# Casting values in the load and packing keys-times-values in 64x64 quadrants: one change to a fused linear-attention and highway kernel

## The chip, the cores and the metric

The kernel runs on one NeuronCore of a Trainium2 chip. Five engines work beside each other and meet at semaphores: PE (TensorE, the matrix array, with its weight loads as PEld), DVE (VectorE), ACT (ScalarE), POOL (GpSimd) and SP (SyncE, which here only issues transfers). The metric is the device time in microseconds (us) of one execution. The kernel before takes 144.22 us, the median of three runs (143.59 to 144.29). The profile comes from one more execution.

## The reference, cut to what matters

```python
# q, k, v: (8 batches, 8 heads, 576 positions, 64), float32
q_s = exp(q - max over the last axis);  q_s /= sum over the last axis
k_s = exp(k - max over positions);      k_s /= sum over positions
kv  = einsum('bhsd,bhse->bhde', k_s, v)          # one 64x64 matrix for each head
x   = einsum('bhsd,bhde->bhse', q_s, kv)         # laid out as 4608 tokens x 512
H   = max(x @ w_h, 0);  T = 1 / (1 + exp(-(x @ w_t + b_t)))
out = T * H + (1 - T) * x                        # 4608 x 512, float32
```

The maxima cancel in the quotients, so the kernel takes plain exponentials and divides by sums that come out of the matrix products through a column of ones.

## The kernel before, in words

All work is written as short steps, and one long string, `ORDER`, gives the order in which they are issued. `v_2_0_4` is a step `v` for batch 2, starting at head pair 0, four pairs. A suffix chooses the engine (`:A` ACT, `:D` DVE, `:P` POOL; `th_9_0:S` writes in place). There is no scheduler behind it: an engine does its steps in the order of the string, and a step that waits holds up all that follows on that engine. The queue in which SP issues transfers goes in the same order.

For each of the eight batches:

- `k`, `v`, `q` load float32 values through SP (lines 168 and 174), into three buffers for each kind. Keys and values have 64 positions of one head on 64 partitions and 9 further positions (`NJ`) along the row, so two heads fill 128 partitions.
- `ek` (line 222, ACT) takes the exponential of the keys into fp16. `vc` (line 227, on ACT, DVE or POOL) copies the values to fp16 into `v16`, where each position has 64 values and, behind them, a one.
- `kv` (line 243, PE) makes keys times values: 144 products with 64 rows, 32 columns of weights and 65 moving columns. Even and odd key channels are separate products, so that each half lands on the 32 partitions that belong to its head. The result `kvps` is in the PSUM tile pool `ps_x`, which has one buffer; the products `xu` use the same buffer.
- `kr` and `kn` (lines 250 and 253, DVE) take the reciprocal of the sums and write the normalised matrix as fp16 into `kvb`.
- `eq` (line 260, ACT) takes the exponential of the queries, `tr` (line 278, DVE) transposes it in 32x32 blocks, `xu` (lines 291 and 301, PE) multiplies by `kvb` for a group of tokens, and `rs` and `x` (lines 313 and 319, DVE) divide by the sums and write the tokens as fp16.

For each of 36 tiles of 128 tokens: `xt` turns the tile on PE (line 326), `xe` copies it out (line 332, ACT or DVE), `bw` puts the bias into a PSUM bank (line 339 by ACT, line 341 by PE), `mt` and `mh` are four products each of 128x128 weights by 512 columns (lines 346 and 352), `th` is the tanh (lines 359 and 362, ACT), `dd`, `uu` and `oo` are the elementwise end (lines 366, 377 and 380, 392, on DVE or POOL), `gg` (line 371, POOL) prepares `uu` on POOL, and `st` and `st1` store (lines 401 and 413).

`fill` (line 155) issues products on an empty tile at the start, so that PE is busy while data is on its way. `setuppool` builds two identity matrices on POOL.

Of the kernel before, what the change touches and what calls it, by code (L numbers as in the profile page):

```python
# [16 lines left out]
b_32 b_0 setupdve fill_10 bsplit v_0_3_1 bp fill_10 v_0_0_1 v_0_2_1 vc_0_0_1:A bc vc_0_3_1:D k_0_2_2 ek_0_2_2 k_0_0_2  # L17
v_0_1_1 q_0_0_8 ek_0_0_2 vc_0_2_1:D bw_1_0 vc_0_1_1:D kv_0 w_t_0 wtc_0:P q_0_8_10 w_h_0 w_t_2 kr_0 eq_0_0_8 tr_0_0_8
w_h_2 kn_0 fill_4 xu_0 rs_0 x_0 setuppool bw_0_0 fill_4 xt_0 whd_1:D eq_0_8_10 whd_0:P tr_0_8_8 xe_0:A xt_1 wtc_2:P
k_1_0_2 xe_1:D whc_0:A xu_1 whd_2:D whd_3:P whc_2:A mt_1_0 th_1_0 mt_0_0 rs_1 x_1 xt_2 ek_1_0_2 v_1_2_2 xe_2:D  # L20
vc_1_2_2:P mh_0 dd_0 mh_2 th_0_0 gg_0_0:P mh_1 bw_2_0 dd_2 bw_3_0:A gg_1_0:P dd_1 v_1_0_2 k_1_2_2 ek_1_2_2 q_1_0_8
eq_1_0_8 xt_3 xe_3:D mt_2_0 vc_1_0_2:D uu_0_0:P mh_3 q_1_8_10 dd_3 oo_0_0:D mt_3_0 tr_1_0_8 uu_1_0:P oo_1_0:P th_2_0
k_2_0_4 gg_2_0:P kv_1 kr_1 kn_1 eq_1_8_10 tr_1_8_8 v_2_0_4 bw_4_0 th_3_0 uu_2_0:P bw_5_0:A xu_2 rs_2 x_2 xt_4 xu_3
ek_2_0_4 tr_0_16_2 oo_2_0:P gg_3_0:P xe_4:D uu_3_0:P rs_3 tr_1_16_2 x_3 xt_5 mt_4_0 xe_5:A mh_5 q_2_0_18 v_3_0_4
k_3_0_4 th_4_0 vc_2_2_2:D vc_2_0_2:A q_3_0_18 xt_6 oo_3_0:P xu_4 rs_4 gg_4_0:P x_4 q_4_0_18 xe_6:A mt_5_0 mh_4 th_5_0
dd_5 dd_4 xt_8 xe_8:D eq_2_0_8 tr_2_0_8 kv_2 kr_2 kn_2 bw_8_0:A gg_5_0:P mt_8_0 eq_2_8_10 tr_2_8_8 mh_6 bw_6_0:A xt_7
th_8_0 xe_7:D bw_7_0:A xu_5 mt_6_0 rs_5 uu_5_0:P dd_6 x_5 vc_3_0_2:A th_6_0:S v_4_0_4 mt_7_0 uu_6_0:D k_4_0_4 mh_7
dd_7 uu_4_0:P xu_6 rs_6 xt_10 xe_10:D th_7_0 oo_5_0:P ek_3_0_4 mh_8 mh_10 x_6 oo_4_0:P dd_8 xt_9 xe_9:D bw_10_0:A
mt_10_0 vc_3_2_2:P kv_3 dd_10 v_5_0_4 eq_3_0_8 tr_3_0_8 kr_3 oo_6_0:P gg_7_0:P uu_7_0:P eq_3_8_10 tr_3_16_2 bw_11_0:A
kn_3 oo_7_0:P xt_11 xe_11:A tr_2_16_2 mh_9 gg_8_0:P uu_8_0:P th_10_0 gg_10_0:P tr_3_8_8 xu_7 bw_9_0:A oo_8_0:P  # L30
eq_4_8_10 vc_4_2_2:P mt_11_0 th_11_0 mt_9_0 th_9_0:S q_5_0_18 uu_10_0:P bw_12_0:A k_5_0_4 rs_7 vc_4_0_2:P dd_9 x_7
eq_4_0_8 xt_12 xe_12:D mh_11 uu_9_0:D oo_9_0:P xu_8 rs_8 gg_11_0:P oo_10_0:P xt_13 xe_13:D dd_11 uu_11_0:P st_0
mt_12_0 xt_14 th_12_0 x_8 mh_12 gg_12_0:P bw_13_0:A mh_13 ek_4_0_4 xu_9 oo_11_0:P mt_13_0 th_13_0:S xe_14:D dd_12 rs_9
xt_15 x_9 q_6_0_18 bw_14_0 xe_15:A dd_13 kv_4 uu_12_0:P oo_12_0:P tr_4_0_8 k_6_0_4 kr_4 vc_5_0_2:A xt_16 xe_16:A
mt_14_0 uu_13_0:D mh_15 kn_4 xu_10 bw_16_0:A th_14_0 gg_14_0:P st_1 tr_4_8_8 dd_15 xt_17 mh_14 rs_10 xe_17:D eq_5_8_10
mt_16_0 vc_5_2_2:P v_6_0_4 bw_15_0:A mt_15_0 x_10 xt_18 dd_14 eq_5_0_8 tr_5_0_8 xu_11 th_16_0 bw_17_0 th_15_0:S
# [5 lines left out]
rs_14 mh_20 tr_6_8_8 th_22_0 oo_16_0:P bw_24_0:A xt_25 st1_17_0 oo_19_0:P gg_22_0:P x_14 gg_20_0:P dd_20 bw_21_0:A
uu_18_0:P st_6 vc_6_0_2:A mt_24_0 th_24_0 xe_25:D tr_6_0_8 mt_21_0 th_21_0:S kv_6 kr_6 uu_21_0:D kn_6 mh_22 dd_22
mh_25 dd_25 xu_15 ek_7_0_4 uu_20_0:P rs_15 x_15 bw_23_0:A mt_23_0 oo_18_0:P eq_7_0_8 tr_7_0_8 uu_22_0:P xt_26 mh_24
bw_25_0:A mt_25_0 st_8 dd_24 th_23_0 xu_16 gg_23_0:P rs_16 xe_26:A xt_28 xe_28:D bw_26_0:A mt_26_0 gg_24_0:P
vc_7_2_2:A oo_21_0:P vc_7_0_2:A x_16 oo_20_0:P st_7 th_25_0:S th_26_0 uu_25_0:D mh_23 gg_26_0:P xt_27 xe_27:A
eq_7_8_10 st_11 kv_7 oo_22_0:D kr_7 kn_7 uu_24_0:P mh_28 dd_23 dd_28 xt_29 mh_26 dd_26 xu_17 rs_17 xe_29:A xt_30
bw_29_0:A mt_29_0 x_17 bw_28_0:A oo_25_0:P mt_28_0 xe_30:A th_29_0 uu_23_0:P oo_24_0:P mh_27 oo_23_0:P st_10 tr_7_8_8
bw_27_0:A uu_26_0:P th_28_0:S uu_28_0:D xt_31 xe_31:A tr_7_16_2 dd_27 mt_27_0 bw_31_0:A th_27_0:S xt_32 xu_18
tr_6_16_2 rs_18 xe_32:A uu_27_0:D gg_29_0:P mt_31_0 x_18 oo_26_0:P th_31_0 mh_29 dd_29 mh_30 bw_30_0:A mt_30_0  # L50
oo_28_0:D bw_32_0:A st_13 oo_27_0:P st_12 uu_29_0:P gg_31_0:P dd_30 th_30_0:S xu_19 rs_19 oo_29_0:P uu_30_0:D
# [8 lines left out]
def kernel(  # L60
# [10 lines left out]
    nc = tc.nc  # L71
# [14 lines left out]
    ldv = pool("ldv", 3)  # L86
# [75 lines left out]
    def load_kv(which):  # L162
        src, p = (k, ldk) if which == "k" else (v, ldv)

        def step(e, b, c, n):
            t = landing(which, b, p).rearrange("p (c f) -> p c f", c=4)
            rows = src[b].rearrange("(c hh) (p j) d -> (hh p) c (j d)", hh=2, p=NP)
            nc.sync.dma_start(t[:, c:c + n], rows[:, c:c + n])  # L168
        return step
# [49 lines left out]
    def ek(e, b, c, n):  # L219
        t = once(f"ek{b}", lambda: ekp.tile([P, NJ, 4, D], FP16, tag="ek", name=f"ek_{b}"))  # L220
        src = T[f"k32{b}"].rearrange("p (c j d) -> p c j d", c=4, j=NJ)
        nc.scalar.activation(t[:, :, c:c + n].rearrange("p j c d -> p c j d"), src[:, c:c + n], AF.Exp)  # L222

    def vc(e, b, c, n):
        copy = dict(A=nc.scalar.copy, D=nc.vector.tensor_copy, P=nc.gpsimd.tensor_copy)[e or "P"]
        src = T[f"v32{b}"].rearrange("p (c j d) -> p c j d", c=4, j=NJ)
        copy(v16[b % NV][:, c:c + n, :, 0:D], src[:, c:c + n])  # L227

    def kv_of(b):
        return T[f"kvps{b}"][:, 0:2, 0:130].rearrange("p m (c e) -> p m c e", c=2)  # L230

    def kv(e, b):


        ps = T[f"kvps{b}"] = ps_x.tile([P, 4, DM], FP32, tag="xu", name=f"kv_{b}")
        for turn in range(2):
            for c in range(2):
                for j in range(NJ):
                    for g in range(4):
                        h = 4 * c + g  # L240
                        hh, i, m = h % 2, h // 2, (turn + h) % 2
                        rows, cols = slice(64 * hh, 64 * hh + 64), slice(32 * g, 32 * g + 32)
                        nc.tensor.matmul(  # L243
                            ps[cols, m, 65 * c:65 * c + 65], T[f"ek{b}"][rows, j, i, m:D:2],
                            v16[b % NV][rows, i, j, 0:65], start=(j == 0), stop=(j == NJ - 1),
                            skip_group_check=True, tile_position=(64 * hh, 32 * g))
# [208 lines left out]
```

## Time and profile before

| | value |
|---|---|
| median of three runs | 144.22 us |
| the profiled execution's own time | 142.23 us |
| its span, first to last instruction | 140.5 us |
| busy: PE, DVE, ACT, POOL | 112.2, 98.2, 90.9, 85.9 us |
| mean granted PE clock | 0.907 |
| read from HBM, written | 30.41 MB, 9.44 MB |
| keys times values (line 243), 1152 products | 12.5 us |
| casts of the values (line 227): ACT, POOL, DVE | 7.5, 5.7, 5.8 us |

The profile page cuts the span into 40 slices of 3.5 us. A digit of an engine's row is its busy share in tenths, PEclk is the clock that the throttle granted to TensorE, and DMA is the busy share of the 16 transfer engines. The chain of work is followed back from the last instruction, at each step to what released it; a piece of it called issue is time in which the engine waited for nothing that the profile names. In the groups of instructions, the last column is the idle time of the engine just before them and what ended it.

### The profile page before, as it was taken

To read this page: it belongs to the slowest core of one execution; us is meant where nothing else is said; L and a number is where in the kernel's file an instruction comes from. 1 tells how busy PE (TensorE), PEld (TensorE's weight loads), DVE (VectorE), ACT (ScalarE), POOL (GpSimd) and SP (SyncE) were. 2 spreads that over 40 slices of the span, in tenths; PEclk is the share of its full clock that TensorE was granted. 3 is DMA by queue.
4 is the path that set the end of the run, shared out by engine and by line. 5 is a ranking of instruction groups with operands and counts; after the bars stand their busy time and mean duration, and the time that the engine had idled before them with its cause. 6 is when DMAs were issued, how large, how long until landed. Compare 5 with 4: busy or idle time off the path is not lost.

```text
span 140.5 us, 5171 instructions
## 1 busy us (share of the span) xinstructions
PE 112.2 (80%) x2267; PEld 58.9 (42%) x2267; DVE 98.2 (70%) x176; ACT 90.9 (65%) x121; POOL 85.9 (61%) x93
## 2 busy tenths in 40 slices
PE   6947879936997599189923999399999999999930
PEld 2315245524364255035522456145565464544510
DVE  3703786977477597557923498287999999998890
ACT  3345376776577595916931689349999978866710
POOL 0001546999139469494980437903998879989930
PEclk9997899996599999959995599869999999999996
DMA  4999999999999999999999999100291052724362
GB/s 138 261 398 407 401 392 387 394 395 398 392 396 410 394 387 392 403 402 405 396 401 399 404 396 355 40 0 0 82 398 53 5 201 103 296 84 167 132 269 106
DMA packets 14890, 40.17 MB, mean 286 GB/s; under 512 B 914, under 2 KB 1170, under 8 KB 14868
## 3 DMA queue, kind: packets, MB, share of 16 engines
q1 hardware_dynamic: 14576, 39.59, 73.9%
q8 instruction: 17, 0.28, 0.8%
q10 hardware_dynamic: 292, 0.27, 0.6%
q14 instruction: 5, 0.04, 0.1%
HBM read 30.41 MB, written 9.44 MB: 284 GB/s over the span
## 4 chain that ended last, share of the span: by engine, by line
PE 63%; DVE 13%; issue 10%; DMA 6%; ACT 3%; SPq 2%; DVEq 0%
PE tps L346 22%; PE gps L352 21%; PE turned L326 7%; PE kv L243 7%; DMA v<-in_v_dram 6%; PE xu L291 4%; DVE d L366 3%; DVE et L278 3%; DVE x L319 2%; ACT qe L260 2%; DVE o L392 2%; SPq L168 2%; DVE v L227 1%; PE turned L155 1%; DVE xT L332 1%
## 5 line engine op out<-in xcount | busy, mean ns | idle before, releaser
L392 POOL TENSOR_TENSOR o<-u,x 128x512 f32<-128x512 f16 (+1 forms) x30 | 35.6, 1195 | 7.4 <-DVE u L377 6.8
L346 PE MATMUL tps<-w16t,xT 128*128 128x512 f16 (+1 forms) x148 | 39.7, 403 | 0.2 <-DVE xT L332 0.2
L352 PE MATMUL gps<-w16h,xT 128*128 128x512 f16 x144 | 38.5, 400 | 0.0
L380 POOL TENSOR_TENSOR u<-g,d 128x512 f16<-128x512 f16 x23 | 27.7, 1212 | 4.7 <-DVE d L366 4.2
L366 DVE SCALAR_TENSOR_TENSOR d<-x,gps 128x512 f16<-128x512 f16 x36 | 24.3, 679 | 4.8 <-PE gps L352 4.7
L371 POOL TENSOR_SCALAR g<-th 128x512 f16<-128x512 f16 x23 | 14.1, 618 | 20.3 <-ACT th L362 20.3
L260 ACT ACTIVATE qe<-q 128x1024 f16<-128x1024 f32 (+1 forms) x16 | 18.6, 1164 | 6.3 <-DVE kvb L253 1.9
L319 DVE TENSOR_TENSOR x<-xu,rs 128x1024 f16<-128x1024 f32 (+1 forms) x20 | 22.2, 1112 | 0.3
L278 DVE STREAM_TRANSPOSE et<-qe 128x512 f32<-128x512 f32 (+1 forms) x24 | 20.0, 835 | 2.9 <-ACT qe L260 2.9
L243 PE MATMUL kv<-v,ek 64*32 64x65 f16 x1152 | 12.5, 197 | 10.3 <-issue 7.3
L346 PEld LDWEIGHTS <-xT 128*128 128x128 f16 x148 | 14.0, 104 | 15.0 <-issue 3.7
L352 PEld LDWEIGHTS <-xT 128*128 128x128 f16 x144 | 13.8, 102 | 14.7 <-issue 2.8
L222 ACT ACTIVATE ek<-k 128x2304 f16<-128x2304 f32 (+1 forms) x10 | 17.4, 1736 | 3.5 <-DMA k<-in_k_dram 3.5
L339 ACT COPY tps<-ball 128x512 f32<-128x512 f32 x29 | 16.8, 592 | 3.3 <-DVE d L366 3.1
L362 ACT ACTIVATE th<-tps 128x512 f16<-128x512 f32 x23 | 13.6, 596 | 8.1 <-PE tps L346 8.0
L332 ACT COPY xT<-turned 128x512 f16<-128x512 f16 x18 | 10.6, 586 | 12.8 <-PE turned L326 12.8
L326 PE MATMUL turned<-idh,x 128*128 128x128 f16 x144 | 15.0, 231 | 4.0 <-DVE x L319 3.3
L243 PEld LDWEIGHTS <-ek 64*32 64x32 f16 x1152 | 11.0, 94 | 13.1 <-issue 8.2
L326 PEld LDWEIGHTS <-x 128*128 128x128 f16 x144 | 10.6, 102 | 11.1 <-DVE x L319 4.1
L291 PE MATMUL xu<-kvb,et 32*128 32x65 f16 x512 | 7.8, 197 | 6.9 <-issue 5.1
L359 ACT ACTIVATE tps<-tps 128x512 f32<-128x512 f32 (+1 forms) x14 | 7.7, 550 | 5.8 <-PE tps L346 5.5
L291 PEld LDWEIGHTS <-et 32*128 32x128 f16 x512 | 5.5, 97 | 13.6 <-issue 7.3
(42 smaller groups left out, 82.3 us busy)
## 6 DMA issues: line engine op xcount, KB each, us to landing
out_dram<-o SPq DMA_DIRECT2D x16, 512.0 KB, 5.6
k<-in_k_dram SPq DMA_DIRECT2D x6, 1152.0 KB, 14.5
v<-in_v_dram SPq DMA_DIRECT2D x6, 1152.0 KB, 16.1
q<-in_q_dram SPq DMA_DIRECT2D x6, 1152.0 KB, 15.3
k<-in_k_dram SPq DMA_DIRECT2D x4, 576.0 KB, 9.1
q<-in_q_dram SPq DMA_DIRECT2D x2, 640.0 KB, 12.1
v<-in_v_dram SPq DMA_DIRECT2D x4, 288.0 KB, 4.1
v<-in_v_dram SPq DMA_DIRECT2D x2, 576.0 KB, 11.5
```

What stands on the lines that cost most here:

```text
L222: nc.scalar.activation(t[:, :, c:c + n].rearrange("p j c d -> p c j d"), src[:, c:c + n], AF.Exp)
L243: nc.tensor.matmul(ps[cols, m, 65 * c:65 * c + 65], T[f"ek{b}"][rows, j, i, m:D:2], v16[b % NV][rows, i, j, 0:65], start=(j == 0), stop=(j ...
L260: nc.scalar.activation(t[:, :, j * D:(j + n) * D], src[:, :, j * D:(j + n) * D], AF.Exp)
L278: nc.vector.transpose(dst, src)
L291: nc.tensor.matmul(t[:, g, col:col + 65], turned_q(bs[0], c, m, 256 * J + P * a, P)(rows), kvb[bs[0] % NKV][rows, m, c, 0:65], start=(m == ...
L319: nc.vector.tensor_mul(dst[:, :, 0:n], sums(u)[:, :, :, 0:64], T[f"rs{u}"][:, :, 0:n].unsqueeze(3).to_broadcast([P, 4, n, D]))
L326: nc.tensor.matmul(t[:, n], x_of(i)[:, n0 + n % 2:n0 + 2 * P:2], idh, is_transpose=True, start=True, stop=True, skip_group_check=True)
L346: nc.tensor.matmul(T[f"tps{i}_{h}"][:, cs], T[f"xT{i}"][:, n], w16["t"][:, n, cs], start=False, stop=(n == 3), skip_group_check=True)
L352: nc.tensor.matmul(t, T[f"xT{i}"][:, n], w16["h"][:, n], start=(n == 0), stop=(n == 3), skip_group_check=True)
L366: nc.vector.scalar_tensor_tensor(t, x_of(i), -0.5, T[f"gps{i}"], op0=ALU.mult, op1=ALU.max)
L380: nc.gpsimd.tensor_mul(t[:, cs], T[f"g{i}_{h}"][:, cs], T[f"d{i}"][:, cs])
L392: eng.tensor_add(t[:, cs], T[f"u{i}_{h}"][:, cs], x_of(i)[:, cs])
```

## The change

Values are no longer loaded as float32 by SP and cast by a compute engine. POOL issues their loads itself, and the transfer writes fp16 straight into `v16`, of which there are now three. A row of `v16` holds the values of all positions, and at its end one block of 64 ones.

`kv` takes whole 64x64 quadrants: 72 products for a batch, each with 64 columns of weights and 128 moving columns, the 64 values of a position and the block of ones. To that end `ek` writes each position's even channels first and its odd ones behind them. Half of each result now lies on the neighbouring 32 partitions. After `kn`, the new step `kp` moves those halves by two products with a permutation matrix `swap` into a further bank of the same PSUM buffer, `kc` (ACT, once DVE) copies them to `kvm`, and `xu` takes each half from `kvb` or `kvm`. `perm` builds `swap` on POOL, ahead of the first load of values.

The order of all steps is new, loads and stores included. On PE the program shrinks from 4536 to 3418 instructions. Nine loads of values stand in POOL's order among its compute steps. Of the other choices of engine, `xe` has three more on ACT, `bw` two more on ACT in place of PE, `oo` one more on DVE in place of POOL, and a weight cast moves from POOL to ACT.

```diff
-b_32 b_0 setupdve fill_10 bsplit v_0_3_1 bp fill_10 v_0_0_1 v_0_2_1 vc_0_0_1:A bc vc_0_3_1:D k_0_2_2 ek_0_2_2 k_0_0_2
...
+q_0_8_10 b_0 b_32 eq_0_8_10 setupdve fill_10 bsplit setuppool perm k_0_0_2 k_0_2_2 ek_0_2_2 bp fill_12 bc bw_3_0
+v_0_2_2 tr_0_8_8 v_0_0_2 q_0_0_8 ek_0_0_2 kv_0 kr_0 kn_0 bw_2_0:A w_h_0 w_t_2 wtc_2:P eq_0_0_8 tr_0_0_8 fill_4 kp_0
+kc_0:A xu_1 rs_1 whd_0:D x_1 fill_5 xt_2 w_t_0 wtc_0:A xu_0 w_h_2 k_1_0_2 xe_2:D rs_0 k_1_2_2 xt_3 x_0 mt_2_0 whd_2:D
...
-    ldv = pool("ldv", 3)
-    NKV, NV = 3, 2
+    NKV, NV = 3, 3
-    v16 = [consts.tile([P, 4, NJ, 66], FP16, name=f"v16_{i}") for i in range(NV)]
+    kvm = [consts.tile([P, 2, 66], FP16, name=f"kvm{i}") for i in range(NKV)]
+    swap = consts.tile([P, 2, P], FP16, name="swap")
+    v16 = [consts.tile([P, 4 * NJ * D + D], FP16, name=f"v16_{i}") for i in range(NV)]
...
+    def perm(e):
+        nc.gpsimd.memset(swap, 0.0)
+        for to in range(4):
+            r, w = 32 * (to ^ 1), to % 2
+            nc.gpsimd.tensor_copy(swap[r:r + 32, w, 32 * to:32 * to + 32], idh[r:r + 32, r:r + 32])
...
-            nc.vector.memset(t[:, :, :, 64:66], 1.0)
+            nc.vector.memset(t[:, 4 * NJ * D:], 1.0)
...
+    def load_v(e, b, c, n):
+        w = NJ * D
+        t = v16[b % NV][:, c * w:(c + n) * w].rearrange("p (c f) -> p c f", c=n)
+        nc.gpsimd.dma_start(t, rows_of(v, b)[:, c:c + n])
...
     def ek(e, b, c, n):
-        t = once(f"ek{b}", lambda: ekp.tile([P, NJ, 4, D], FP16, tag="ek", name=f"ek_{b}"))
-        src = T[f"k32{b}"].rearrange("p (c j d) -> p c j d", c=4, j=NJ)
-        nc.scalar.activation(t[:, :, c:c + n].rearrange("p j c d -> p c j d"), src[:, c:c + n], AF.Exp)
-
-    def vc(e, b, c, n):
-        copy = dict(A=nc.scalar.copy, D=nc.vector.tensor_copy, P=nc.gpsimd.tensor_copy)[e or "P"]
-        src = T[f"v32{b}"].rearrange("p (c j d) -> p c j d", c=4, j=NJ)
-        copy(v16[b % NV][:, c:c + n, :, 0:D], src[:, c:c + n])
+        t = once(f"ek{b}", lambda: ekp.tile([P, 4 * NJ, D], FP16, tag="ek", name=f"ek_{b}"))
+        src = T[f"k32{b}"].rearrange("p (s r m) -> p s r m", s=4 * NJ, m=2)
+        dst = t.rearrange("p s (m r) -> p s r m", m=2)
+        at = slice(NJ * c, NJ * (c + n))
+        nc.scalar.activation(dst[:, at], src[:, at], AF.Exp)
...
-        for turn in range(2):
-            for c in range(2):
-                for j in range(NJ):
-                    for g in range(4):
-                        h = 4 * c + g
-                        hh, i, m = h % 2, h // 2, (turn + h) % 2
-                        rows, cols = slice(64 * hh, 64 * hh + 64), slice(32 * g, 32 * g + 32)
-                        nc.tensor.matmul(
-                            ps[cols, m, 65 * c:65 * c + 65], T[f"ek{b}"][rows, j, i, m:D:2],
-                            v16[b % NV][rows, i, j, 0:65], start=(j == 0), stop=(j == NJ - 1),
-                            skip_group_check=True, tile_position=(64 * hh, 32 * g))
+        for c in range(2):
+            for j in range(NJ):
+                for g in range(4):
+                    hh, i, col = g % 2, 2 * c + g // 2, 64 * (g // 2)
+                    rows = slice(64 * hh, 64 * hh + 64)
+                    at = (NJ * i + j) * D
+                    moving = bass.AP(vt.tensor, vt[rows, at:at + D].offset,
+                                     [list(vt[rows].ap[0]), [4 * NJ * D - at, 2], [1, D]])
+                    nc.tensor.matmul(
+                        ps[col:col + 64, hh, 128 * c:128 * c + 128], T[f"ek{b}"][rows, NJ * i + j],
+                        moving, start=(j == 0), stop=(j == NJ - 1),
+                        skip_group_check=True, tile_position=(64 * hh, col))
...
+    def kp(e, b):
+        for w in range(2):
+            nc.tensor.matmul(T[f"kvps{b}"][:, 2, 0:130].rearrange("p (c e) -> p c e", c=2), swap[:, w],
+                             kvb[b % NKV][:, w, :, 0:65], start=(w == 0), stop=(w == 1), skip_group_check=True)
+
+    def kc(e, b):
+        copy = nc.vector.tensor_copy if e == "D" else nc.scalar.copy
+        copy(kvm[b % NKV][:, :, 0:65], T[f"kvps{b}"][:, 2, 0:130].rearrange("p (c e) -> p c e", c=2))
+
+    def kv_rows(b, g, c, m):
+        rows = slice(32 * g, 32 * g + 32)
+        return kvb[b % NKV][rows, m, c, 0:65] if m == g % 2 else kvm[b % NKV][rows, c, 0:65]
...
-                                kvb[bs[0] % NKV][rows, m, c, 0:65], start=(m == 0), stop=(m == 1),
+                                kv_rows(bs[0], g, c, m), start=(m == 0), stop=(m == 1),
```

More of the change, by code (lines that the diff above doesn't have):

```diff
@@ L22 @@
[L22 to L36, printed above, removed]
@@ L42 @@
[L42 to L51, printed above, removed]
@@ new lines @@
+k_6_0_4 dd_9 tr_4_8_8 th_14_0 kv_4 kr_4 xe_17:D kn_4 ek_5_0_4 mt_9_0 gg_14_0:P xt_15 xe_15:A v_6_0_4 kp_4 oo_12_0:P
+st_6 kc_4:A mh_17 th_9_0:S xt_16 tr_4_0_8 bw_17_0:A dd_17 uu_9_0:D kv_5 kr_5 kn_5 bw_13_0:A mt_17_0 xe_16:D bw_15_0:A
+kp_5 th_17_0:S eq_5_8_10 oo_9_0:P kc_5:D uu_14_0:P mt_13_0 tr_4_16_2 uu_17_0:D oo_17_0:P xu_10 rs_10 x_10 tr_5_16_2
+mt_15_0 th_13_0 gg_13_0:P tr_5_8_8 mh_13 dd_13 st_2 xt_19 bw_16_0:A mt_16_0 xu_14 rs_14 x_14 th_15_0 oo_14_0:P mh_15
+dd_15 eq_5_0_8 uu_13_0:P oo_13_0:P mh_16 dd_16 xe_19:A th_16_0 gg_16_0:P uu_16_0:P xu_11 rs_11 x_11 xt_18 mh_19
@@ new lines @@
+mt_24_0 xe_23:A uu_26_0:D x_15 mt_25_0 oo_21_0:P th_24_0 uu_20_0:P gg_24_0:P eq_7_0_8 tr_7_0_8 oo_20_0:P st1_17_0
+th_25_0 gg_25_0:P mh_23 mh_24 dd_23 bw_23_0:A xu_16 ek_7_0_4 rs_16 xt_27 xe_27:D st_8 dd_24 mt_23_0 th_23_0:S mh_25
+st_5 mh_27 x_16 xt_28 uu_23_0:D dd_25 st_10 kv_7 xe_28:A xt_30 st_7 oo_26_0:P bw_28_0:A mt_28_0 dd_27 uu_24_0:P kr_7
+mh_28 uu_25_0:P kn_7 eq_7_8_10 bw_27_0:A th_28_0 xe_30:D kp_7 oo_23_0:D kc_7:A xt_22 xe_22:A bw_22_0:A st1_26_0
+mt_27_0 th_27_0:S dd_28 xu_17 tr_7_8_8 st_11 rs_17 oo_24_0:P oo_25_0:P st_13 uu_27_0:D xt_29 xe_29:A mt_22_0 th_22_0
@@ L56 @@
+oo_31_0:P bw_35_0 st_17 oo_33_0:P st_18 mt_35_0 th_35_0:S mh_35 dd_35 uu_35_0:D bw_35_1 mt_35_1 th_35_1:S uu_35_1:D
+oo_35_0:D st1_35_0:A oo_35_1:D st1_35_1:A
 """
@@ L160, in landing, with rows_of, load_k @@
         return once(f"{which}32{b}", lambda: p.tile([P, H * S * D // P], FP32, tag=which, name=f"{which}32_{b}"))
[L162 to L169, printed above, removed]
+    def rows_of(src, b):
+        return src[b].rearrange("(c hh) (p j) d -> (hh p) c (j d)", hh=2, p=NP)
+    def load_k(e, b, c, n):
+        t = landing("k", b, ldk).rearrange("p (c f) -> p c f", c=4)
+        nc.sync.dma_start(t[:, c:c + n], rows_of(k, b)[:, c:c + n])
+    def load_v(e, b, c, n):
+        w = NJ * D
+        t = v16[b % NV][:, c * w:(c + n) * w].rearrange("p (c f) -> p c f", c=n)
+        nc.gpsimd.dma_start(t, rows_of(v, b)[:, c:c + n])
     def load_q(e, b, j, n):
@@ L302, in xu @@
                             t[64 * w:64 * w + 64, g, 65 * c:65 * c + 65], turned_q(b, c, m, 512, 64)(rows),
-                            kvb[b % NKV][rows, m, c, 0:65], start=(m == 0), stop=(m == 1),
+                            kv_rows(b, g, c, m), start=(m == 0), stop=(m == 1),
                             skip_group_check=True, tile_position=(32 * g, 64 * w))
```

43 lines of the change are left out of this document (27 added, 16 removed).

## The prediction

> **What bounds the kernel now.** I read the page first: busy times, slices, queues.
>
> ```profile
> PE 112.2 (80%) x2267; PEld 58.9 (42%) x2267; DVE 98.2 (70%) x176; ACT 90.9 (65%) x121; POOL 85.9 (61%) x93
> ...
> PEclk9997899996599999959995599869999999999996
> DMA  4999999999999999999999999100291052724362
> ...
> q8 instruction: 17, 0.28, 0.8%
> ```
>
> PE is busiest. The loads keep the transfer engines full until slice 25, 87 us, and then there is room. The clock falls to half in several slices of that loaded stage and in none after slice 28 but the last. The chain of waits in order of time says why:
>
> ```profile
> 44.56 0.23 PE xu L291 x16
> 44.79 2.43 issue
> 47.22 0.30 PE xu L291 x16
> ...
> 57.16 0.36 PE xu L291 x24
> 57.52 2.64 issue
> 60.16 0.30 PE xu L291 x8
> ...
> 69.89 1.24 PE kv L243 x139
> 71.13 4.72 issue
> 75.85 0.29 PE kv L243 x4
> ...
> 86.28 1.26 PE kv L243 x133
> 87.54 2.61 issue
> 90.15 0.21 PE kv L243 x3
> ```
>
> From 33 to 131 us the chain is PE, with four holes, together 12.40 us, in the middle of runs of small products whose data is there. Counted in PE's own stream, the work resumes at instructions 1470, 1982, 2494 and 3004, 510 to 512 apart, and the packets of queue 8 (17 of 16,384 bytes, kind "instruction") land at 45.83, 58.84, 74.57 and 88.81 us: each hole ends 1.3 to 1.4 us after one. So PE runs out of program. Seventeen packets for 4536 instructions is 256 or so to a packet, and the spacing of the holes is two packets. From entering one block of 256 to the start of the next packet takes 3.3 to 4.0 us while loads run and 1.0 to 1.5 us just after them. The shortest blocks under load last 5.7 to 6.1 us, whatever is in them. One batch of kv is 288 instructions that need 1.28 us.
>
> The stage sums show what PE does without holes:
>
> ```profile
> 70.00:80.00 10.00, 5.28 (x156) 2.61 (x141) 3.39 (x6) 4.21 (x7) 3.91 (x5) 0.67 1.04 402
> ...
> 110.00:120.00 10.00, 10.00 (x255) 5.71 (x254) 9.31 (x15) 8.63 (x14) 9.26 (x10) 1.00 0.28 108
> ```
>
> Columns after the length: busy PE, PEld, DVE, ACT, POOL, then clock, DMA share and rate. From 70 to 80 us everything starves; from 110 to 120 us PE is full at full clock while DVE is at 93% and POOL at 93%. The other engines can follow a PE without holes.
>
> **The change part by part.** The sum is against the profiled execution (142.23 us: span 140.5 and 1.7 around it). The median of the runs is 144.22, so 2.0 are added at the end.
>
> *Holes and clock.* The four holes are 12.4 us. After three of them the clock was at half: 59.7 to 63.1, 73.4 to 80.2 and 90.5 to 93.9 us. PE was busy for 3.0, 4.4 and 3.4 us of those and would have needed half: 5.4 lost. Together -17.8.
>
> *Holes that remain.* The new stream has 3418 instructions, 1118 fewer, kv being 144 a batch. I cut it into blocks of 256 at the same offset (PE stands still at 190 plus multiples of 256) and priced each by rows: 0.216 us for a 512-column product, 0.055 for a turning one, 0.36 for xu, 1.3 for kv. Blocks 1 to 10 then need 3.9, 5.8, 6.6, 6.7, 6.1, 4.8, 7.1, 7.4, 8.8 and 5.3 us; before, blocks 4, 6, 8 and 10 needed 3.0, 2.2, 1.1 and 1.1. Against 6.0 us a block the short ones miss 2.1, 0.2, 1.2 and 0.7: 4.2, of which I take 4.0, the last lying where loads end. Bounds 0 (waits for data lie in the same time) and 6 (with a clock spell): +4.0.
>
> *A second queue of loads.* A packet of program now waits behind two streams. The loads added about 2.5 us to its start; a second stream may add nothing or as much again. Blocks 2 to 7 at 8.5 us would lose 2.7, 1.9, 1.8, 2.4, 3.7 and 1.4, less the 1.4 already counted in two of them: 12.5. Values are a third of the bytes loaded, so I take a third: +4.2, bounds 0 and 12.5.
>
> *kv itself.* Before, four tiles of the array at a time: 144 products in 1.28 us are 35.6 ns for a round of four, each 65 moving columns. Now a round has 128 columns and 64 of weights in place of 32. Twice the round for half the rounds is 1.28 us again. Below: 18 rounds at 55 ns (a 128-column turning product) are 0.99, or -2.3 over eight batches. Above: 72 products one after another at 55 ns are 3.96, or +21.4. Row line 243 shows tiles of the same rows working together (35.6 ns is less than two products), so I stay with 0.
>
> *kp, kc.* kp has 16 products of 130 columns: 16 x 0.055 = +0.9. kc by slope of line 359 (580 ns for 512, 368 for 256) is about 0.26 us; ACT gets 7 of them. Between kn and xu now stand kp, kc and two handovers, some 0.5 us, while xu's buffer is held. From the second batch on other PE work (mt, mh or xt) is issued between kv, kp and xu and covers it; in batch 0 only fills do: +0.5. Uncovered in all eight, 4.
>
> *Casts removed.* ACT loses 7.5 us, POOL 5.7, DVE 5.8. Two casts are in the chain, both on DVE, 0.77 at 10.86 and 1.17 at 25.29 us: -1.9. In return the first load of values moves from SP at 0.74 us behind POOL's identities (1.0 us by their rows) and perm (memset and four copies, 0.7 by similar rows), to about 2.7: +2.0. SP's queue starts with q and k at once, which ek and eq need anyway. ACT with three more xe (0.59), two more bw (0.59), kc and a weight cast ends near 89 us busy, DVE near 94, POOL near 78 and the issues. ek writes its output in halves; if that doubled its 0.83 ns per element, ACT would have 15 us more, of 50 idle: 0.
>
> *POOL's issues.* Six of the nine loads are issued between tile work on POOL (v_2 to v_7), and all that POOL has behind them waits: gg, uu, oo, then the stores on SP, and the loads of q and k behind those stores (st_6 stands ahead of q_7 and k_7). The nearest rows are SP's: an issue of k or v has a median of 0.54 us, and under load up to 5.59 (at 40.16 us). POOL's 74.6 us of work after 24 us fit into a span of 132 with 14 us to spare at the 85% it reached from 94 to 131 us, and 22 at 93%: 2.3 to 3.7 us an issue. I take 2 us: 0 on the path. [...]
>
> *Transfers.* Bytes read stay the same, at 397 GB/s. Five stores now stand ahead of the last loads, 2.6 MB or 6.6 us, but from 87 us on the engines were idle, and kv_7 ran at 113: 0 here, unless the cast slows them.
>
> Sum: -17.8 + 4.0 + 4.2 + 0.9 + 0.5 - 1.9 + 2.0 = -8.1. Profiled 134.1, median 136.1.
>
> **The rivals.**
>
> *Program or loads wait longer.* If the second queue costs the full 12.5 in place of 4.2, the time is 144.4. The same comes if the cast halves the rate of the values: 9.44 MB at 397 GB/s are 23.8 us more, loads end near 111, kv_7 cannot run before 113, as now: 144. For: 3.3 to 4.0 us for a packet in one queue. Against: the same bytes flow. [...]
>
> *POOL becomes the bound: slower.* The place is v_2 to v_7 on POOL. Beyond some 3 us each, every further us costs 6 us; the gain of 8.1 is gone at 4.4 us. At SP's worst, 5.6 us, it is 15.6 more: 151.7. [...] Against: SP's long issues fall where transfers queue behind each other. [...]
>
> *Quadrants do not overlap.* kv takes 3.96 us: +21.4, and as its blocks then outlast the packets the 8.2 of program waits go: 149.3. From about 3.3 us per kv it is slower. Against: the row above.
>
> **How the numbers follow.** Forecast 0.60, own range 128 (no second-queue cost, half of the remaining holes, the low end of kv) to 142 (6 us of holes; kp and kc uncovered). Longer waits 0.17, POOL 0.15, quadrants 0.08. A measurement of this kernel can tell about 0.5% from no change. Of the second case a third is faster, a third within that, a third slower: faster 0.66, same 0.05, slower 0.29. The range 126 to 151 reaches to the rivals and leaves about 0.08 on each side.
>
> **What would show it.** Right: some 13 packets of queue 8; no piece of issue over 2.5 us on PE under load; the clock at half only at the start and once more; kv near 1.3 us a batch; POOL idle behind its issues for about 2 us. Wrong: holes of 2 us at every 256 instructions (second queue); idle POOL before gg, uu or oo beyond 3 us at each load (issues); kv above 3 us; loads still running past 95 us; PE waiting for kvm.

## The result and the profile after

The changed kernel takes 197.64 us, the median of four runs (196.85 to 198.63), against 143.91 us for the kernel before (143.47 to 144.29): a ratio of 1.374, 95% interval 1.364 to 1.383. It is slower by 53.7 us. The profiled execution took 198.63 us, its span is 196.8.

The page of the changed kernel, busy times, slices of 4.9 us and queues:

```profile
PE 121.7 (62%) x1708; PEld 64.6 (33%) x1708; DVE 95.1 (48%) x172; ACT 152.7 (78%) x126; POOL 85.3 (43%) x99
...
ACT  2699439974999499369999995799969999774730
...
PEclk9975699757696695599985856999669995799996
DMA  5999999990850999039401998104900540023326
...
q0 software_dynamic: 4240, 4.72, 14.9%
q8 instruction: 13, 0.21, 0.4%
```

DVE and POOL do about as much as before (98.2 and 85.9 us). ACT has grown from 90.9 to 152.7 us and is now the busiest engine. PE's clock is at half in many slices, all along the kernel, and the loads, which kept the transfer engines full until 87 us, now come in bursts. So something holds all engines up, and it has to do with ACT. The groups of instructions name it (busy time, mean ns of one, then the idle time of the engine ahead of them and what ended it):

```profile
L236 ACT ACTIVATE ek<-k 128x2304 f16<-128x2304 f32 (+1 forms) x10 | 84.1, 8458 | 1.7 <-DMA k<-in_k_dram 1.7
...
L397 POOL TENSOR_SCALAR g<-th 128x512 f16<-128x512 f16 x23 | 14.1, 618 | 64.5 <-ACT th L388 64.4
L255 PE MATMUL kv<-v,ek 64*64 64x128 f16 x576 | 16.9, 308 | 39.5 <-ACT ek L236 39.5
...
L262 DVE RECIPROCAL rz<-kv 128x4 f32<-128x4 f32 x8 | 1.5, 182 | 45.3 <-PE kv L255 45.3
```

The first line is the exponential of the keys: 84.1 us in ten instructions. In the kernel before, the tile `ek` shows the same ten, shortest, median and longest in ns:

```profile
L222 ACT ACTIVATE ek<-k x10: 1154/2116/2125, 8.6 to 104.7; 128x2304 f16<-128x2304 f32 x6, 128x1152 f16<-128x1152 f32 x4
```

and in the kernel after:

```profile
L236 ACT ACTIVATE ek<-k x10: 5321/10470/10504, 8.0 to 155.0; 128x2304 f16<-128x2304 f32 x6, 128x1152 f16<-128x1152 f32 x4
```

Same elements, same types, five times the duration: six of 2.12 us and four of 1.16 were 17.4 us, and are 84.1. The other three groups show who stands still meanwhile. PE waits 39.5 us for `ek` itself, DVE 45.3 us for PE's `kv`, and POOL 64.4 us for `th`, an ACT instruction that in ACT's order often stands behind an `ek`. In the kernel before, POOL's wait for `th` was a third of that:

```profile
L371 POOL TENSOR_SCALAR g<-th 128x512 f16<-128x512 f16 x23 | 14.1, 618 | 20.3 <-ACT th L362 20.3
```

The chain of work that ended last runs through `ek` for 23% of the span; in order of time one of them looks like this:

```profile
93.59 0.59 ACT tps L365
94.19 10.40 ACT ek L236
104.58 0.04 issue
104.63 2.13 PE kv L255 x72
```

The 72 products behind it take 2.13 us: PE had nothing to do for 8.3 us, and its granted clock from 104.6 to 106.8 us is 0.50.

What differs in the instruction is its pattern. It runs through the keys in order, two neighbours at a time, and writes the even one into the first half of its position and the odd one 32 elements, 64 bytes, behind it. Each element that it writes lies 64 bytes on from the one before, or 62 bytes back.

### The profile page after: what moved, and what is told of

The parts are those of the page before. It is cut to its first block, busy times and chain, and to the rows that moved or that the text cites. A ratio compares the mean times of both kernels' runs of the same rounds, so it can differ in the third digit from the quotient of the medians.

```text
span 196.8 us, 4049 instructions
## 1 busy us (share of the span) xinstructions
PE 121.7 (62%) x1708; PEld 64.6 (33%) x1708; DVE 95.1 (48%) x172; ACT 152.7 (78%) x126; POOL 85.3 (43%) x99
## 3 DMA queue, kind: packets, MB, share of 16 engines
q1 hardware_dynamic: 10288, 30.15, 41.5%
HBM read 30.41 MB, written 9.44 MB: 202 GB/s over the span
## 4 chain that ended last, share of the span: by engine, by line
ACT 33%; PE 32%; issue 18%; DVE 8%; DMA 3%; POOL 3%; SPq 0%; DVEq 0%; ACTq 0%; POOLq 0%
ACT ek L236 23%; PE tps L372 10%; PE kv L255 8%; PE gps L378 8%; DMA k<-in_k_dram 3%; PE turned L352 3%; ACT th L388 3%; DVE x L345 2%; ACT tps L365 2%; DVE d L392 2%; ACT xT L358 2%; POOL o L418 2%; ACT tps L385 1%; DVE u L403 1%; PE xu L317 1%
## 5 line engine op out<-in xcount | busy, mean ns | idle before, releaser
L236 ACT ACTIVATE ek<-k 128x2304 f16<-128x2304 f32 (+1 forms) x10 | 84.1, 8458 | 1.7 <-DMA k<-in_k_dram 1.7
L372 PE MATMUL tps<-w16t,xT 128*128 128x512 f16 (+1 forms) x148 | 42.0, 417 | 0.8 <-ACT xT L358 0.4
L397 POOL TENSOR_SCALAR g<-th 128x512 f16<-128x512 f16 x23 | 14.1, 618 | 64.5 <-ACT th L388 64.4
L255 PE MATMUL kv<-v,ek 64*64 64x128 f16 x576 | 16.9, 308 | 39.5 <-ACT ek L236 39.5
L418 POOL TENSOR_TENSOR o<-u,x 128x512 f32<-128x512 f16 x29 | 34.1, 1187 | 12.6 <-DVE u L403 11.9
L255 PEld LDWEIGHTS <-ek 64*64 64x64 f16 x576 | 15.1, 168 | 43.2 <-ACT ek L236 41.3
L262 DVE RECIPROCAL rz<-kv 128x4 f32<-128x4 f32 x8 | 1.5, 182 | 45.3 <-PE kv L255 45.3
L286 ACT ACTIVATE qe<-q 128x1280 f16<-128x1280 f32 (+1 forms) x16 | 18.4, 1161 | 3.4 <-DMA q<-in_q_dram 2.2
L365 ACT COPY tps<-ball 128x512 f32<-128x512 f32 x31 | 19.3, 634 | 0.9 <-DVE d L392 0.4
L358 ACT COPY xT<-turned 128x512 f16<-128x512 f16 x21 | 12.6, 602 | 6.9 <-PE turned L352 6.9
L403 DVE SCALAR_TENSOR_TENSOR u<-tps,d 128x512 f16<-128x512 f32 (+1 forms) x14 | 9.0, 648 | 17.9 <-ACT tps L385 15.8
```

Source lines behind the costliest of these rows:

```text
L236: nc.scalar.activation(dst[:, at], src[:, at], AF.Exp)
L255: nc.tensor.matmul(ps[col:col + 64, hh, 128 * c:128 * c + 128], T[f"ek{b}"][rows, NJ * i + j], moving, start=(j == 0), stop=(j == NJ - 1), ...
L365: nc.scalar.copy(t[:, cs], ball[:, cs])
L372: nc.tensor.matmul(T[f"tps{i}_{h}"][:, cs], T[f"xT{i}"][:, n], w16["t"][:, n, cs], start=False, stop=(n == 3), skip_group_check=True)
L418: eng.tensor_add(t[:, cs], T[f"u{i}_{h}"][:, cs], x_of(i)[:, cs])
```

## The experiments

### The exponential by halves

The changed kernel with one edit: the same result in the same place, but the loop runs over the 32 even channels and then over the 32 odd ones. It reads every second element and writes 32 in a row.

```diff
-        src = T[f"k32{b}"].rearrange("p (s r m) -> p s r m", s=4 * NJ, m=2)
-        dst = t.rearrange("p s (m r) -> p s r m", m=2)
+        src = T[f"k32{b}"].rearrange("p (s r m) -> p s m r", s=4 * NJ, m=2)
+        dst = t.rearrange("p s (m r) -> p s m r", m=2)
```

> The changed kernel with one edit: ek runs through each position by halves (32 even channels, then 32 odd ones), so that it reads every second element and writes 32 in a row, where the changed kernel reads in a row and writes pairs 64 bytes apart. The result in memory is the same. Theory A (the 10.49 us of an ek are the price of writing pairs apart, and they alone make the kernel slow): ek falls to about 2.1 us, ACT's busy time from 152.7 to about 86 us, and the time to what the prediction's sum gave, 136 us (126 to 145). Rival B (any pattern that is not in a row on both sides costs that much on ACT): ek stays at 8 to 10 us, the time within 5 us of 197. Rival C (something else in the change made it slow, the ek only fills waits): ek falls, the time stays above 160 us.

Measured: 128.69 us (127.27 to 128.91) against 144.14, ratio 0.898 (0.889 to 0.907). The page of that kernel:

```profile
PE 104.6 (83%) x1708; PEld 55.7 (44%) x1708; DVE 94.2 (75%) x172; ACT 87.6 (69%) x126; POOL 85.1 (67%) x99
...
PEclk9999756999999999999999999999999999999995
...
q8 instruction: 13, 0.21, 0.6%
```

ACT has lost 65.1 us of work and the span 70.4. The exponential of 128x2304 takes 2.31 us:

```profile
L236 ACT ACTIVATE ek<-k x10: 1223/2306/2335, 8.5 to 93.7; 128x2304 f16<-128x2304 f32 x6, 128x1152 f16<-128x1152 f32 x4
```

Theory A holds: the order in which `ek` is written costs the whole loss and more, and the rest of the change makes the kernel faster by a tenth. The clock is at half for a moment early on, then full until the last slice.

### The kernel before with the slow writes

The kernel before with nothing of the change but the pattern: `ek` is written as in the changed kernel, and `kv` reads its weights from the halves. Values, quadrants and order are the old ones.

```diff
-        src = T[f"k32{b}"].rearrange("p (c j d) -> p c j d", c=4, j=NJ)
-        nc.scalar.activation(t[:, :, c:c + n].rearrange("p j c d -> p c j d"), src[:, c:c + n], AF.Exp)
+        src = T[f"k32{b}"].rearrange("p (s r m) -> p s r m", s=4 * NJ, m=2)
+        dst = t.rearrange("p s (m r) -> p s r m", m=2)
+        at = slice(NJ * c, NJ * (c + n))
+        nc.scalar.activation(dst[:, at], src[:, at], AF.Exp)
...
-                            ps[cols, m, 65 * c:65 * c + 65], T[f"ek{b}"][rows, j, i, m:D:2],
+                            ps[cols, m, 65 * c:65 * c + 65], T[f"ek{b}"].rearrange("p j c d -> p (j c) d")[rows, NJ * i + j, 32 * m:32 * m + 32],
```

> The kernel before with one part of the change: ek writes even channels first and odd ones behind them, as pairs 64 bytes apart, and the keys-times-values products read these halves in a row. Loads, casts, products and order are those of before. Theory A: ek takes 10.5 us a batch here too, 8.4 more than before, ACT's busy time goes from 91 to about 158 us, and the time rises to 180 to 205 us. Rival D (ek is slow in the changed kernel because of something beside it, such as loads issued by POOL): ek stays at 2.1 us and the time at 144 us.

Measured: 201.64 us (199.96 to 202.38) against 144.14, ratio 1.404 (1.390 to 1.419). Its page:

```profile
PE 124.4 (62%) x2267; PEld 63.9 (32%) x2267; DVE 97.9 (49%) x176; ACT 156.8 (78%) x121; POOL 85.4 (43%) x93
...
L225 ACT ACTIVATE ek<-k 128x2304 f16<-128x2304 f32 (+1 forms) x10 | 84.1, 8462 | 1.4 <-DMA k<-in_k_dram 1.4
```

The same 84.1 us without a casting load on POOL, without quadrants and in the old order. So the slow `ek` does not come from other new work beside it, as rival D had it: it belongs to the instruction.

### What in the pattern costs: seven orders

Seven exponentials and three copies, each 128x2304 from float32 to fp16, behind the last work of the kernel before, where nothing runs beside them.

```diff
+            (f, o),
+            (two(f, "p s r m"), half(o, "p s r m")),
+            (two(f, "p s m r"), half(o, "p s m r")),
+            (half(f, "p s r m"), two(o, "p s r m")),
+            (half(f, "p s m r"), two(o, "p s m r")),
+            (f.rearrange("p (s r m) -> p s r m", s=36, m=4), o.rearrange("p (s m r) -> p s r m", s=36, m=4)),
+            (f.rearrange("p (s r m) -> p s r m", s=36, m=8), o.rearrange("p (s m r) -> p s r m", s=36, m=8)),
...
+            nc.scalar.activation(dst, src, AF.Exp)
```

> The kernel before with ten extra instructions on one 128x2304 tile behind its last step, seven exponentials on ACT and three copies on DVE, f32 to f16; only their own durations count. In order on ACT: in a row on both sides; written as pairs 64 bytes apart; read at every second element and written in a row by 32; read as pairs 128 bytes apart and written in a row; read in a row by 32 and written at every second element; written as pairs replaced by fours 32 bytes apart; by eights 16 bytes apart. DVE does the first three. The first two runs gave 10.5 and 2.3 us for the second and third pattern. Theory A1 (writes that jump cost, reads do not): 2.1, 10.5, 2.3, 2.1, then well over 2.1 for every second element. Theory A2 (an innermost run of two costs, on either side): 2.1, 10.5, 2.3, 10.5, 2.3, and fours and eights in proportion to the number of runs, about 6 and 4. [...] DVE: if its copy of pairs stays near its first, the cost is ACT's own.

The first four on ACT in the timeline (start, duration):

```profile
139.55 2.12 ACT L433 ACTIVATE ek<-k 128x2304 f16<-128x2304 f32 x1 [2.79 <-issue]
141.71 10.40 ACT L433 ACTIVATE ek<-k 128x2304 f16<-128x2304 f32 x1
152.14 2.24 ACT L433 ACTIVATE ek<-k 128x2304 f16<-128x2304 f32 x1
154.41 2.60 ACT L433 ACTIVATE ek<-k 128x2304 f16<-128x2304 f32 x1
```

| read | written | ACT, us | DVE, us |
|---|---|---|---|
| in a row | in a row | 2.12 | 1.36 |
| in a row | pairs 64 bytes apart (the change) | 10.40 | 5.71 |
| every second element | rows of 32 | 2.24 | 1.36 |
| pairs 128 bytes apart | in a row | 2.60 | |
| in a row | every second element, 4 bytes on | 2.78 | |
| in a row | fours, 32 bytes apart | 9.86 | |
| in a row | eights, 16 bytes apart | 10.29 | |

The same pairs that cost 10.40 us to write cost 2.60 to read, and groups of two, four and eight cost the same. So it is the distance between one written element and the next, and not the shortness of the inner run. Theory A2 falls with the 2.60 us. Theory A1 comes nearest, though pairs cost a little to read (it had 2.1) and every second element, with 2.78 us, costs less than it had. DVE pays four times as well, so the cost is not ACT's alone.

### How far apart is too far

The same place, ten exponentials with one step each, and three copies on DVE.

```diff
+        def wr(step, inner, t=o):
+            n = 2304 // (step * inner)
+            return (f.rearrange("p (s r m) -> p s r m", s=n, m=inner), t.rearrange("p (s m r) -> p s r m", s=n, m=inner))
...
+        src, dst = (wr(2, 32), wr(4, 16), wr(6, 16), wr(8, 16), wr(32, 72), rd(4, 16), rd(32, 72),
+                    wr(2, 32, T["q327"]), wr(4, 16, T["q327"]), wr(32, 2, T["q327"]))[which]
```

> Ten exponentials on ACT and three copies on DVE over 128x2304 elements behind the kernel before, as in the last run of patterns, where a step of 4 bytes between elements written one after another cost 2.78 us in all and steps of 16, 32 and 64 bytes 10.29, 9.86 and 10.40. Steps of the writes, f16: 4, 8, 12, 16 and 64 bytes (the last with 72 in a row, where it was pairs before); then reads at steps of 16 and 128 bytes written in a row; then f32 written at steps of 8 and 16 bytes and as pairs 128 bytes apart. DVE: f16 written at steps of 4, 8 and 16 bytes. Theory L (a jump of 16 bytes or more between writes costs, whatever the number of elements in a row): 2.8 at 4 bytes, about 10 at 16 and 64, somewhere between at 8 and 12; reads 2.3 to 2.6; f32 10 at 16 and 128 bytes, and at 8 as f16 at 8. Theory M (only elements of two bytes suffer): f32 near 2.3 throughout.

ACT in the timeline: fp16 written at steps of 4, 8, 12 and 16 bytes, float32 read at 16 bytes, float32 written at 8 and 16 bytes:

```profile
141.13 2.79 ACT L432 ACTIVATE ek<-k 128x2304 f16<-128x2304 f32 x1 [2.79 <-issue]
143.95 5.27 ACT L432 ACTIVATE ek<-k 128x2304 f16<-128x2304 f32 x1
149.25 7.85 ACT L432 ACTIVATE ek<-k 128x2304 f16<-128x2304 f32 x1
157.13 10.40 ACT L432 ACTIVATE ek<-k 128x2304 f16<-128x2304 f32 x1
...
177.79 4.25 ACT L432 ACTIVATE ek<-k 128x2304 f16<-128x2304 f32 x1
...
186.06 2.30 ACT L432 ACTIVATE q<-k 128x2304 f32<-128x2304 f32 x1
188.39 4.40 ACT L432 ACTIVATE q<-k 128x2304 f32<-128x2304 f32 x1
```

At 64 bytes, 72 in a row, it is 10.20 us, and for float32 in pairs 128 bytes apart 4.31. So the cost of an fp16 write grows by some 2.5 us for each 4 bytes from 4 to 16 bytes, and no further. For fp16 writes that is what theory L expected. For float32 writes both theories miss: at 16 bytes L had 10 us and M near 2.3, and it is 4.40; at 8 bytes it is 2.30. Reads at long steps cost 4.1 to 4.3 us, where L had 2.3 to 2.6. The tile view has the three of DVE, steps of 4, 8 and 16 bytes:

```profile
L430 DVE CAST ek<-k x3: 1491/2764/5343, 186.2 to 190.5; 128x2304 f16<-128x2304 f32 x3
```

At the same step the two types differ: at 8 bytes float32 takes 2.30 us and fp16 5.27, at 16 bytes 4.40 and 10.40. No run shows why.

### Fewer products in the kernel before

The next two kernels test the step of the forecast that carried the gain, that PE runs out of program. The first is the kernel before, with `kv` over five of the nine positions: 80 products a batch in place of 144, everything else untouched.

```diff
-                for j in range(NJ):
+                for j in range(0, NJ, 2):
```

> The kernel before with 5 of the 9 products of each sum in keys times values: the sums run over fewer positions, so 4 of 9 positions are left out of the result. PE's stream loses 1024 of its 4536 instructions, about what the change takes off, and nothing else moves. Theory E (PE waits for its program while loads run): no hole of over 2.5 us in the chain under load, 13 or 14 instruction packets; the holes and the half clock behind them give 12 to 18 us and the shorter products another 3: 144 falls to 124 to 132 us. Rival F (the holes only show a time that the loads or the other engines need anyway): 140 to 143 us.

Measured: 126.31 us (124.34 to 128.48) against 144.14 (142.07 to 145.68); the fastest runs of the two lie 17.7 us apart. The page:

```profile
PE 102.7 (83%) x1755; PEld 52.4 (42%) x1755; DVE 97.3 (78%) x176; ACT 90.0 (72%) x121; POOL 85.7 (69%) x93
...
PEclk9997699999558999999999999999999999999999
...
q8 instruction: 13, 0.21, 0.7%
```

17.8 us less, while the work left out is 64 of 144 products, some 0.6 of 1.28 us a batch, 4.6 us in all; that leaves some 13 for the holes and the half clock behind them. Thirteen packets of program come in place of 17, and one hole is left in the chain:

```profile
74.37 2.04 issue
```

It stands, like the holes of the kernel before, at a multiple of 256 instructions in PE's stream, counted from them. The next longest pieces of issue are 0.83 and 0.56 us. The holes went with the instructions, as theory E has it.

### Quadrants alone, in the old order

The kernel before with its own order, its float32 loads of values on SP and its casts, and of the change only the quadrants, the block of ones, `kp` and `kc`, with `ek` written by halves.

```diff
-h_2 kn_0 fill_4 xu_0
+h_2 kn_0 fill_4 kp_0 kc_0:A xu_0
...
-    v16 = [consts.tile([P, 4, NJ, 66], FP16, name=f"v16_{i}") for i in range(NV)]
+    v16 = [consts.tile([P, 4 * NJ * D + D], FP16, name=f"v16_{i}") for i in range(NV)]
...
+        w = NJ * D
+        copy(v16[b % NV][:, c * w:(c + n) * w], T[f"v32{b}"][:, c * w:(c + n) * w])
```

> The kernel before, in its own order, with the quadrants alone: 72 products of 64x64 and 128 columns a batch, the block of ones, kp and kc after each kn, ek by halves; values are still loaded by SP as float32 and cast by vc, and POOL builds its identities at the start. Theory E (holes in PE's program are most of what the change gains): PE's stream shrinks by a quarter, no hole over 2.5 us, 126 to 133 us. Rival G (the gain comes from taking casts off the engines or from the new order): 138 us or more.

Measured: 131.04 us (129.93 to 133.22) against 143.67, ratio 0.911 (0.902 to 0.921). Its page:

```profile
PE 105.7 (83%) x1707; PEld 55.6 (43%) x1707; DVE 97.4 (76%) x176; ACT 92.4 (72%) x129; POOL 87.0 (68%) x98
...
PEclk9999999999779999999999999999999999999996
...
q8 instruction: 13, 0.21, 0.7%
```

The longest piece of issue in its chain is 0.82 us, where the kernel before has four of 2.4 to 4.7. In PE's own stream no pause of over 0.25 us stands at one of those places, multiples of 256 instructions apart. With quadrants alone the holes are gone, and 12.6 us with them. Theory E holds again, and rival G falls.

### Casting loads, in the old order

The kernel of the last experiment, and POOL's casting loads in place of SP's loads and the casts; the old order, with `v` where it was.

```diff
-    ldv = pool("ldv", 3)
-    NKV, NV = 3, 2
+    NKV, NV = 3, 3
...
+        nc.gpsimd.dma_start(t, rows_of(v, b)[:, c:c + n])
...
-    def vc(e, b, c, n):
```

> The quadrants in the old order, with POOL's casting loads as well: no vc, three fp16 buffers, each load where the order before has it, now in POOL's queue. What differs from the changed kernel with ek by halves is the order alone, and from the quadrants in the old order the loads alone. Theory J (casting loads take 19 us of casts off three engines and cost POOL 0.8 us an issue; the first values land about 5 us later): within 3 us of the quadrants with SP's loads. Rival K (the casting loads slow the other loads or the program's packets): over 4 us more than those.

Measured: 142.15 us (141.00 to 143.64) against 143.67, ratio 0.991 (0.986 to 0.997). That is 11 us more than with SP's loads, where expectation J had 3 at most. The chain in order of time shows where:

```profile
4.88 10.86 DMA v<-in_v_dram
...
15.78 2.13 PE kv L255 x64
...
29.21 9.25 DMA v<-in_v_dram
...
38.51 2.16 PE kv L255 x60
```

and POOL's timeline what its second load stood behind:

```profile
28.06 1.20 POOL L397 TENSOR_SCALAR g<-th 128x512 f16<-128x512 f16 x2 [9.44 <-ACT th L388]
29.21 0.74 POOL L180 DMA_DIRECT2D v<-in_v_dram  x1
29.98 1.17 POOL L406 TENSOR_TENSOR u<-g,d 128x512 f16<-128x512 f16 x1
```

The second half of batch 1's values is issued at 29.21 us, behind a `gg` that waited 9.44 us for ACT. It lands 9.25 us later, and `kv` of batch 1 starts at 38.5 us; in the kernel before, with SP's loads, it starts at 27.2. From there on nothing is lost: between the same two points of PE's program, ten packets apart, the two kernels take 79.8 us each (45.17 to 124.98, and 33.30 to 113.08). So under way neither the casting loads nor the casts that they save show in the time; the loads are late when POOL, whose queue they stand in, is late.

To separate the two I moved only the first loads of values in that kernel: batch 0's ahead of the identities, in two loads in place of four, and batch 1's whole behind the first weight cast, in one load in place of two.

```diff
-b_32 b_0 setupdve setuppool perm
+b_32 b_0 setupdve v_0_0_2 v_0_2_2 setuppool perm
...
-w_t_0 wtc_0:P q_0_8_10
+w_t_0 wtc_0:P v_1_0_4 q_0_8_10
```

> The quadrants and POOL's casting loads in the old order, as in the run before that took 142.15 us, with the loads of the first two batches of values earlier in POOL's queue: batch 0 ahead of the identities, batch 1 whole behind the first weight cast (before, its second half stood behind two gg at 29.2 us, and PE waited for it until 38.5). Theory N (the 11 us that this kernel lost on the quadrants with SP's loads lie in its first 38 us, in values that POOL issued late): 131 to 135 us. Rival K (casting loads slow the loads or the program all along): 139 us or more.

Measured: 132.51 us (131.28 to 133.16) against 144.08, ratio 0.923 (0.913 to 0.933). The 11 us are back but for 1.5, and those are not clear of noise: the intervals of the two ratios overlap (0.902 to 0.921 with SP's loads). Theory N, the place of the first loads, holds; K, a standing cost of the casting loads (139 us or more), falls.

### The faster version with its first values earlier

The kernel by halves, with batch 0's values issued ahead of the identities and the permutation.

```diff
-q_0_8_10 b_0 b_32 eq_0_8_10 setupdve fill_10 bsplit setuppool perm k_0_0_2 k_0_2_2 ek_0_2_2 bp fill_12 bc bw_3_0
-v_0_2_2 tr_0_8_8 v_0_0_2
+q_0_8_10 b_0 b_32 eq_0_8_10 setupdve v_0_0_2 v_0_2_2 fill_10 bsplit setuppool perm k_0_0_2 k_0_2_2 ek_0_2_2 bp fill_12
+bc bw_3_0 tr_0_8_8
```

> The changed kernel with ek by halves (128.69 us in its run, where the first kv began at 16.15 us, waiting for values, and at 11.31 in the kernel before), with one more edit: POOL issues the two loads of the first values before it builds the identities and the permutation, 2.4 us earlier. Theory H (the start is set by when these loads enter the shared engines): kv begins near 13 us and the time falls by 1.5 to 4 us, to 125 to 127. Rival I (their share of the engines beside SP's loads sets it, or later work takes up the slack): 128 to 129.5 us.

Measured: 126.60 us (126.02 to 128.01) against 143.67, ratio 0.881 (0.873 to 0.890), the fastest of the kernels that leave nothing out. That is 2.1 us less than the kernel by halves, as theory H had it, though the intervals of the two ratios touch. In the kernel by halves the first `kv` hung on the values, with the chain

```profile
4.10 12.01 DMA v<-in_v_dram
...
16.15 2.13 PE kv L255 x67
```

Here it starts behind `ek`:

```profile
12.62 2.14 PE kv L255 x67
```

This kernel and the one of the experiment before it differ in the string of the order alone: 126.60 against 132.51. The new order, with the engines that it chooses, is worth about 5.9 us. PE's waits show where most of it lies: how long PE waited in all, how often, and the longest time, in the old order

```profile
PE kv L271 <- DVE kvb L265: 3.9, 4, 1.9
PE xu L317 <- ACT kvm L276: 1.8, 4, 0.7
```

and in the new one, where it never waits for `kvb`:

```profile
PE xu L317 <- ACT kvm L276: 0.4, 1, 0.4
```

The first line is `kp` waiting for `kn`, the others are `xu` waiting for `kc`. In the old order little or no other work of PE stands between these steps; the new one puts more of it between `kv`, `kp` and `xu`.

## Why the prediction was wrong

The forecast was 136.1 us and 0.66 for faster; the kernel takes 197.64. The step that failed stands under "Casts removed": "ek writes its output in halves; if that doubled its 0.83 ns per element, ACT would have 15 us more, of 50 idle: 0". Both halves of it are wrong.

- *The price.* It measured 4.40 ns an element by the same reckoning, the slope between 10.49 us for 2304 and 5.42 for 1152: five times and not twice, 66.7 us more in all. The doubling was a bound without a row: no ACT instruction of the kernel before writes each element away from the last, so nothing in its trace shows ACT's price. The nearest row is `tr` on DVE, which writes float32 16 bytes apart and takes 1.10 us for 512 elements, and no row there shows it in a row to compare with. So the bound should have stayed open upwards.
- *The cover.* ACT's idle time was 49.6 us before (140.5 less 90.9), and it hid nothing: against the kernel by halves ACT has 65.1 us more to do, and the span is 70.4 us longer. Each engine does its steps in order here, so its idle time is made of waits for others: `ek` stands ahead of `th`, `xe`, `bw` and `eq`, and while it runs PE, then DVE and POOL come to a stop. That ACT comes out as the bound was not among the rivals.

The rest of the sum can be held against the kernel by halves, which differs from the changed one in that loop alone. The sum gave 134.1 us for a profiled execution; it took 128.14. The runs split the change into steps, each the difference of two medians:

| part | forecast, us | measured, us | between the medians |
|---|---|---|---|
| quadrants, `kp`, `kc`, fewer instructions | -12.4 | -12.6 in the old order | 143.67 and 131.04 |
| the new order | none | -5.9 | 132.51 and 126.60 |
| casting loads; first values late | +4.3 | +1.5; +2.1 | 131.04 and 132.51; 126.60 and 128.69 |
| how `ek` is written | 0 | +69.0 | 128.69 and 197.64 |

`ek` apart, that is -15 us where the sum has -8.1. The first row agrees by luck: the sum is for the new order.

- *Holes and clock, -17.8.* Right: thirteen packets, no piece of issue above 0.91 us on the chain until the loads end (1.47 at 106.14 us is the longest in all), mean clock 0.962 in place of 0.907. Quadrants alone gained 12.6 us, with PE waiting 6.3 us around `kp` and `kc` where the kernel before waits 1.7 for `kvb`, and with 0.9 of `kp` itself by the forecast: some 18 without these, an estimate. That taking out 512 products gave 17.8 as well is chance, since some 4.6 of it are those products.
- *Holes that remain, +4.0.* Too much. In the kernel by halves PE pauses at multiples of 256 instructions, just behind a packet, for 0.47 us at 36.20 and 0.39 at 68.68: 0.9 in all. The longer pieces of issue on that chain before 90 us (0.91, 0.79, 0.62, 0.83 and 0.70) are not PE's: they lie within ACT instructions that were running, as 62.23 to 63.02 us within an `ek` from 60.79 to 63.11.
- *A second queue of loads, +4.2.* Wrong, 0 was right. From entering one block of program to the start of the next packet takes 2.4 to 4.7 us, mostly about 3.6, as with one queue (3.3 to 4.0). The term was the author's estimate, a third of what a second wait of 2.5 us would lose in blocks 2 to 7; no run here shows such a second wait, nor what the 2.5 us consist of. Nor did the cast halve the rate: values take 21.9% of the engines' 126.4 us for 9.44 MB read, 2.9 us per MB, and the rest of the loads and stores 63.2% for 30.15 MB, 2.65: a tenth dearer.
- *kv, 0.* Right: 72 products in 1.20 us at full clock, where 1.28 was forecast. The rival of quadrants that don't overlap (3.96) falls.
- *kp and kc, +1.4 together.* Right in the new order, which the term counted on: `kp` takes 0.12 us at full clock and `kc` 0.27, and `xu` waits 0.4 us for `kc` once. ACT waits 9.8 us for `kp` in four places, 7.5 of them in batch 0, where the values are late. In the old order PE waits 5.7 us here, as shown above, which is most of what the new order gains.
- *Casts and start, -1.9 and +2.0.* The start was mis-sized: the first `kv` runs at 16.15 us and not at 11.31, as before: 4.8 later. The forecast had the issue right (3.2 us for 2.7) and left out that the values then need 12.0 us to land, where the first of the kernel before needed 7.7 (later ones take 9.0 to 16.5). The -1.9 for the casts shows in no comparison: casting loads with their first values early gain nothing on SP's loads and the casts (+1.5).
- *POOL's issues, 0 on the path.* Right, with 2 us taken and 0.81 measured (0.72 to 0.91), in a kernel whose DVE is 75% busy. The rival of POOL as the bound falls.
- *What is left.* Without `ek` the sum is 6.9 us too long. The second queue and the holes that remain make 7.3 of it, and the rest of the loads and the start, forecast 3.5 us too low, works against them. That leaves about 3 us open.
- *The reading of the chain.* The prediction has it on PE from 33 to 131 us. From 50.3 to 57.1 us it runs through DVE and ACT; no term hangs on that.

## What to carry to other kernels

When a change turns the order in which an instruction walks through its operand, write down the byte distance between one written element and the next, and let the loop follow the output: in an exponential of 128x2304 on ACT, reading every second float32 cost 0.12 us on 2.12, writing fp16 pairs 64 bytes apart 8.3. Long steps of the reads are not free either: float32 read 16 or 128 bytes apart, one after another, took 4.25 and 4.08 us in place of 2.12. Where the trace has no row for such a price, leave the bound open upwards, and ask what stands behind the instruction on its engine; idle time there is no cover by itself. And a large loss can hide a gain: all of this change but two lines makes the kernel 10% faster, and those two lines make that 54% slower.

## What the runs showed that I had not expected

- An exponential on ACT with an fp16 result costs by the step of its writes: 128x2304 in 2.12 us in a row, 2.79 at 4 bytes, 5.27 at 8, 7.85 at 12 and 9.9 to 10.4 at 16, 32 and 64. DVE: 1.36, then 1.49, 2.76 and 5.34 at 4, 8 and 16 bytes. Float32 results on ACT: 2.30 at 8 bytes, 4.3 to 4.4 at 16 and at 128. Float32 reads at 16 and 128 bytes: 4.25 and 4.08; yet 2.60 when the walk comes back to its neighbours, as pairs 128 bytes apart do, which writes are not spared (10.40). Why writes and reads differ in this is not settled.
- A long wait of PE can be paid twice: behind 8.3 us of it the 72 products take 2.13 us, at a clock of 0.50, in place of 1.20. It is not so each time: behind the first hole of the kernel before, 2.43 us, the clock stayed at 1.0.
- Casting loads take POOL 0.81 us each to issue and no measurable time beside it, but they inherit POOL's queue: the place of the first two batches' loads in it made 9.6 us (142.15 against 132.51).
